# A two-memory attention kernel: a quad's sums stored in one transfer and read back in pieces, with new delays in the instruction plan

## The chip, the cores and the metric

The kernel runs on one core of a Trainium2 chip. A core has a matrix engine (TensorE, PE in the profile, its weight loads PEld), a vector engine (VectorE, DVE), an activation engine (ScalarE, ACT), a general engine (GpSimd, POOL) and SyncE (SP), which here does nothing but issue transfers to the core's 16 DMA engines. Each engine works through its own instruction stream strictly in order, and the streams are tied together by semaphores. The metric is the device time of one execution in microseconds; the median of the runs is given.

## What is computed

Two branches A and B get the same input `x` (2048 tokens, 640 features) with weights of their own. Each is an attention with 32 heads of 20 features over four segments of 512 tokens, together with a memory that is carried from segment to segment. The outputs are mixed by a gate per token.

```python
def _A_ref(x, wq, wk, wv, wo, beta):          # _B_ref is the same with B's weights
    H = 32; Dh = D // H; N = 4; L = S // N
    q, k, v = ...                              # x @ wq, x @ wk, x @ wv, by head and segment
    phi = lambda t: jnp.where(t > 0, t + 1.0, jnp.exp(t))
    mask = (ar[:, None] < ar[None, :]) * (-1e9)
    g = _sigmoid(beta).reshape(1, H, 1, 1)
    for s in range(N):
        logits = jnp.einsum("bhqd,bhkd->bhqk", qs, ks) * scale + mask
        p = _softmax(logits, axis=-1)
        a_dot = jnp.einsum("bhqk,bhkd->bhqd", p, vs)
        num = jnp.einsum("bhld,bhde->bhle", phi(qs), M)
        den = jnp.einsum("bhld,bhd->bhl", phi(qs), z)[..., None] + 1e-6
        outs.append(g * (num / den) + (1.0 - g) * a_dot)
        M = M + jnp.einsum("bhld,bhle->bhde", phi(ks), vs)
        z = z + jnp.einsum("bhld->bhd", phi(ks))
    return o @ wo

g = _sigmoid((x * gate_w).sum(-1, keepdims=True))
return g * a + (1 - g) * b
```

## The kernel before

**Units of work.** The work is cut into eight windows `t`: segment `t // 2` of branch `t % 2`. In a window stand the products of q, k and v with their weights (`job_qk`, `job_v`, 15 terms each, since every factor is split into a high and a low part), and the output product of the window before (`job_o`). All of these are issued on line 748. The 32 heads of a window are taken four at a time: eight quads `u`, 64 quads in all, `i = 8 t + u`. A quad has score products with queries in the rows (`s_unit`, line 1182), whose row maxima VectorE finds (line 1169); the maxima are turned around (line 1207) and written back beside the queries by two small transfers (line 1219). Then come score products with keys in the rows (`t_unit`, line 1272), whose exponentials ScalarE takes (line 1264) and GpSimd masks (line 1265), and the sums over the keys (`pv_unit`, line 1292). All products land in eight PSUM banks, each of which is free again when VectorE or ScalarE has read it. TensorE is used as two halves of 64 rows that work side by side.

**A quad's sums.** `pv_unit` leaves a tile `oT` of 128 rows and 512 tokens: for each of the four heads 20 rows of sums, one row with the sum of the exponentials (the denominator), and 11 rows of no use, 32 rows per head. In windows 0 to 6, `send_dot` writes it to DRAM: the four denominator rows to `dens` (line 1337) and the 20 rows of each head to `dots` (line 1339), five transfers, so that `dots` holds 640 rows without gaps. When half of the heads of a window are there, `reciprocals` reads their denominators back as a tile `dn` (line 1382), VectorE multiplies them with the gates and takes reciprocals (lines 1362 and 1364), and the result goes out (`recs`, line 1367) and is spread to 20 rows per head (`wide`, line 1372). `mix` then reads 128 rows of `dots` (line 1408) and of `wide` (line 1409), multiplies them (line 1406 on VectorE or 1407 on GpSimd) and splits the product for the output product. 35 such mixes are made, five per window.

**What sets the order.** Every engine's order is made when the program is built, by a small event model inside the kernel. It keeps a clock, a ready list per engine sorted by priority, and two numbers for the DMA engines. `put` charges an instruction its duration; `dma` charges SyncE for the issue and calls what comes behind the transfer after an assumed delay:

```python
    def dma(us, emit, then=None, prio=5, lat=1.1, some=False):

        def issued():
            dma_free[0] = max(clk[0] + 0.9, dma_free[0]) + us
            if not some:
                dma_free[0] = dma_free[1] = max(dma_free[0], clk[0] + 0.9 + us, dma_free[1] + us)
            if then:
                at(dma_free[0] + lat, then)

        put("S", 0.37, emit, issued, prio)
```

An instruction is written into its engine's stream when the model says that its inputs are there. If the transfer takes longer on the chip, the engine stands at that instruction, and all that is written behind it waits too. The table `RULES` holds eight settings per quad (the order of score units, how far ahead of the steady work they are spread, and some thresholds). `window_jobs` lists a window's products: `HEAD` holds the first five of the next window (q0, k0, q1, k1, q2); two of them stand ahead of the output products of the window before, three behind.

Weights come in through three tiles `wst` (line 546 for q, k and o, line 522 for v), are rounded by ScalarE (lines 538 and 512) and their low parts taken by GpSimd (lines 540 and 515). Tiles of `x` transposed come in by line 568 (ScalarE reads them on line 558), rows of `x` for the gate by line 613 (VectorE reads them on line 603).

## Time and profile before

| | us |
|---|---|
| runs shown, lowest, median, highest | 1056.81, 1060.92, 1069.14 |
| the profiled execution, its own time | 1060.1 |
| its span, first to last instruction | 1058.4 |
| mean granted TensorE clock | 0.997 |

The profile comes from one execution. An engine's "busy" is the time with at least one instruction in flight. A row of the waits names an engine and the line that stood waiting, what ended the wait, and then the total in us, the number of times and the longest. SyncE's rows ("SPq") give the time in which it issues; when a transfer lands, they don't tell. A row of the chain or of the timeline begins with start and length in us. In a row of windows stand the window, its length, and the busy time of each engine with its count of instructions, then the clock, the share of the DMA engines that is busy, and GB/s. The page counts 1301 transfers issued by SyncE.

### The profile page before, as it was taken

To read this page: it belongs to the slowest core of one execution; us is meant where nothing else is said; L and a number is where in the kernel's file an instruction comes from. 1 tells how busy PE (TensorE), PEld (TensorE's weight loads), DVE (VectorE), ACT (ScalarE), POOL (GpSimd) and SP (SyncE) were. 2 spreads that over 40 slices of the span, in tenths; PEclk is the share of its full clock that TensorE was granted. 3 is DMA by queue.
4 is the path that set the end of the run, shared out by engine and by line. 5 is a ranking of instruction groups with operands and counts; after the bars stand their busy time and mean duration, and the time that the engine had idled before them with its cause. 6 is when DMAs were issued, how large, how long until landed. Compare 5 with 4: busy or idle time off the path is not lost.

```text
span 1058.4 us, 31354 instructions
## 1 busy us (share of the span) xinstructions
PE 1013.3 (96%) x11260; PEld 853.4 (81%) x11260; DVE 768.8 (73%) x2642; ACT 658.2 (62%) x1338; POOL 582.9 (55%) x1016
## 2 busy tenths in 40 slices
PE   9998989899999999899999999999999999999998
PEld 7987877787988878777797888878888787787885
DVE  4777767577786768776778767887577886788864
ACT  6376656747576575656767557665575665658572
POOL 4454546546375563655737357475573644647362
PEclk9999999999999999999999999999999999999999
DMA  7996878787787779876767777887777877878631
GB/s 258 295 287 191 269 226 256 210 253 253 211 264 231 238 226 281 242 224 198 242 197 243 243 237 236 253 263 244 227 233 230 271 222 242 278 209 283 167 123 63
DMA packets 137307, 246.50 MB, mean 233 GB/s; under 512 B 21456, under 2 KB 25584, under 8 KB 137152
## 3 DMA queue, kind: packets, MB, share of 16 engines
q1 hardware_dynamic: 137152, 244.50, 75.6%
q8 instruction: 89, 1.46, 0.6%
q14 instruction: 66, 0.54, 0.2%
HBM read 159.88 MB, written 92.91 MB: 239 GB/s over the span
## 4 chain that ended last, share of the span: by engine, by line
PE 69%; DMA 16%; DVE 4%; ACT 3%; issue 3%; POOL 2%; SPq 2%; DVEq 0%; ACTq 0%; POOLq 0%
PE bank L748 40%; PE bank L1292 10%; PE bank L1182 6%; PE bank L1272 5%; DMA row<-wide 3%; DMA dn<-dens 2%; DMA kd<-row 2%; PE bank L938 2%; PE bank L858 2%; PE bank L898 2%; DMA row<-in_xT_dram 2%; ACT p L1264 1%; DMA qst<-qd 1%; DVE bank L1169 1%; DMA wst<-in_b_wk_dram 1%
## 5 line engine op out<-in xcount | busy, mean ns | idle before, releaser
L1169 DVE CUSTOM_DVE_ANT_0 bank<-bank,tri 128x512 f32<-128x512 f32 (+3 forms) x1024 | 474.4, 520 | 138.2 <-PE bank L1182 117.7
L748 PE MATMUL bank<-row,wh 64*128 64x512 f32 x2308 | 502.6, 403 | 0.1
L1264 ACT ACTIVATE p<-bank 128x512 f32<-128x512 f32 x576 | 316.5, 598 | 133.7 <-PE bank L1272 108.7
L1265 POOL TENSOR_SCALAR_AFFINE_SELECT p<-p 128x256 f32<-128x256 f32 (+1 forms) x576 | 215.6, 384 | 229.8 <-ACT p L1264 219.1
L748 PEld LDWEIGHTS bank<-row,wh 64*128 64x128 f32 x2308 | 320.7, 186 | 13.8 <-issue 1.2
L748 PE MATMUL bank<-row,wl 64*128 64x512 f32 x1154 | 297.1, 401 | 0.0
L540 POOL TENSOR_TENSOR wl<-wst,wh 128x640 fp32r<-128x640 f32 x115 | 179.7, 1566 | 79.5 <-ACT wh L538 75.3
L1182 PE MATMUL bank<-kst,qst 60*128 60x384 f32 (+3 forms) x1024 | 178.3, 320 | 14.7 <-ACT p L1264 5.3
L748 PE MATMUL bank<-wvh,row 64*128 64x320 f32 x1280 | 188.5, 316 | 0.9 <-DVE mx L1169 0.4
L1272 PE MATMUL bank<-qst,kst 62*128 62x512 f32 (+3 forms) x1024 | 174.6, 318 | 14.8 <-DVE mx L1169 5.2
L748 PEld LDWEIGHTS bank<-row,wl 64*128 64x128 f32 x1154 | 173.4, 186 | 5.3 <-issue 0.4
L748 PEld LDWEIGHTS bank<-wvh,row 64*128 64x128 f32 x1280 | 154.0, 186 | 4.8 <-ACT p L1264 1.1
L1182 PEld LDWEIGHTS bank<-kst,qst 60*128 60x128 f32 x1024 | 130.7, 186 | 28.0 <-ACT p L1264 9.2
L1272 PEld LDWEIGHTS bank<-qst,kst 62*128 62x128 f32 x1024 | 130.8, 186 | 24.1 <-DVE mx L1169 6.5
L1292 PE MATMUL bank<-p,vst 128*32 128x256 f32 (+3 forms) x1908 | 144.6, 426 | 1.8 <-DVE mx L1169 1.4
L1169 DVE DVE_READ_ACCUMULATOR2_ANT mx<- 128x1 f32 x1024 | 144.7, 141 | 0.0
L1292 PEld LDWEIGHTS bank<-p,vst 128*32 128x32 f32 x1908 | 59.1, 110 | 86.1 <-issue 62.1
L538 ACT CAST wh<-wst 128x640 fp32r<-128x640 f32 x119 | 87.1, 740 | 40.0 <-PE bank L748 10.5
L748 PE MATMUL bank<-wvl,row 64*128 64x320 f32 x640 | 107.2, 312 | 0.0
L748 PEld LDWEIGHTS bank<-wvl,row 64*128 64x128 f32 x640 | 84.8, 185 | 0.3
L515 POOL TENSOR_TENSOR wvl<-wst,wvh 128x640 fp32r<-128x640 f32 (+1 forms) x48 | 64.0, 1337 | 32.9 <-ACT wvh L512 30.9
L715 DVE TENSOR_TENSOR row<-bank,row 128x512 fp32r<-128x512 f32 x80 | 54.3, 686 | 28.2 <-ACT row L708 14.4
(117 smaller groups left out, 1154.9 us busy)
## 6 DMA issues: line engine op xcount, KB each, us to landing
qd<-row SPq DMA_DIRECT2D x120, 256.0 KB
kd<-row SPq DMA_DIRECT2D x120, 256.0 KB
qst<-qd SPq DMA_DIRECT2D x128, 240.0 KB
kst<-kd SPq DMA_DIRECT2D x128, 240.0 KB
dots<-row SPq DMA_DIRECT2D x224, 40.0 KB
wide<-recs SPq DMA_DIRECT2D x14, 640.0 KB
row<-dots SPq DMA_DIRECT2D x35, 256.0 KB
row<-wide SPq DMA_DIRECT2D x35, 256.0 KB
```

The source lines that it names most:

```text
L515: put("G", 0.77 * n, lambda: nc.gpsimd.tensor_tensor(out=wl[:, a:b, :], in0=w3, in1=r32(wh[:, a:b, :]), op=ALU.subtract), end, prio=4)
L538: put("A", 0.625, lambda: nc.scalar.copy(wh, w3), lambda: put(lo_eng, lo_cost, lambda: lo.tensor_tensor(out=wl, in0=w3, in1=r32(wh), op=AL ...
L540: lambda: lo.tensor_tensor(out=wl, in0=w3, in1=r32(wh), op=ALU.subtract), end, prio=3), prio=6)
L715: put("D", 0.605, lambda: nc.vector.tensor_tensor(out=lo, in0=src, in1=r32(hi), op=ALU.subtract), out, prio=1)
L748: return nc.tensor.matmul(bank_of, lhsT=w[ROWS[half]], rhs=x_[ROWS[half]], start=start, stop=stop)
L858: return nc.tensor.matmul(pm[:, a - h0:c - h0, :].rearrange("p h e -> p (h e)"), lhsT=r32(pqTs[t, m][ROWS[half], P * n:P * (n + 1)]), rhs= ...
L1169: put("D", w / 960.0 + 0.105, lambda: nc.vector.tensor_tensor_reduce(out=sc[:, off:off + w], in0=sc[:, off:off + w], in1=tri[:, L - w:], s ...
L1182: lane_ops[half].append((mm(w), lambda pair=pair, qb=qb, off=off, w=w, r=r, sc=sc: nc.tensor.matmul(sc[:, off:off + w], lhsT=q[r, pair, P ...
L1264: put("A", 0.483, lambda: nc.scalar.activation(pt, sc, AF.Exp, scale=SCALE), lambda: (bank.give(sc), put("G", 0.15 + 0.105 * len(todo), la ...
L1265: "G", 0.15 + 0.105 * len(todo), lambda: nc.gpsimd.affine_select(out=blocks, in_=blocks, pattern=[[0, len(todo)], [1, P]], base=0, channel ...
L1272: lane_ops[half].append((mm(w), lambda pair=pair, kb=kb, off=off, w=w, r=r, sc=sc: nc.tensor.matmul(sc[:, off:off + w], lhsT=k[r, pair, P ...
L1292: nc.tensor.matmul(po[32 * j:32 * j + 32, P * kb:], lhsT=vst[t % 2][:, kb, h * E1:h * E1 + 32], rhs=pts[i, n, f][0][:, off:off + w], start ...
```

## The change

Four things are changed.

1. `send_dot` writes the whole tile `oT`, 128 rows, in one transfer. `dots` has 1024 rows instead of 640 (32 per head), and `dens` is gone; `reciprocals` reads the denominators as every 32nd row of `dots`.
2. `mix` gathers its 128 rows in pieces: one transfer for the whole heads among them, and one for the part of a head at either end. For the five mixes of a window these are 2, 3, 3, 3 and 2 pieces, 13 in place of 5.
3. The model charges an issue 0.44 us in place of 0.37 (0.63 to 0.69 for some kinds), and assumes longer delays: `lat` 2.0 in place of 1.1 for weights, for x tiles of segments 1 to 3, for the token rows and for `dn`, 1.8 for both reads of a mix, 1.6 for the gate rows, 1.4 for `recs`.
4. Three products of the next window stand ahead of the output products, not two. The table `RULES` has new numbers in nearly all of its rows.

```diff
     RULES = {
-        0: "STTSTSSTST 0.902 2.38 0.24 8 0.0 0.78 1",
+        0: "TSTSTSTSTS 1.010 1.98 0.35 8 0.0 1.6 1.92",
...
-    def dma(us, emit, then=None, prio=5, lat=1.1, some=False):
+    def dma(us, emit, then=None, prio=5, lat=1.1, some=False, issue=0.44):
...
-        put("S", 0.37, emit, issued, prio)
+        put("S", issue, emit, issued, prio)
...
-    dots = [dram.tile([D, L], F32, name=f"dots{i}") for i in range(7)]
-    dens = [dram.tile([H, L], F32, name=f"dens{i}") for i in range(7)]
+    dots = [dram.tile([32 * H, L], F32, name=f"dots{i}") for i in range(7)]
...
-        got += ahead[:2]
+        got += ahead[:3]
         if t > 0:
             got += [(t - 1, "o", m) for m in range(KT)]
-        got += ahead[2:]
+        got += ahead[3:]
...
-            dma(0.84, lambda: nc.sync.dma_start(out=w3, in_=src[m]), landed, prio=0 if i < 4 else need[i])
+            dma(0.84, lambda: nc.sync.dma_start(out=w3, in_=src[m]), landed, prio=0 if i < 4 else need[i], lat=1.1 if i < 4 else 2.0)
...
-        one = then_all(5, sent)
-        dma(0.1, lambda: nc.sync.dma_start(out=dens[t][4 * u:4 * u + 4, :], in_=oT[DH::32, :]), one, prio=-1)
-        for j in range(4):
-            dma(0.12, lambda j=j: nc.sync.dma_start(
-                out=dots[t][80 * u + DH * j:80 * u + DH * (j + 1), :], in_=oT[32 * j:32 * j + DH, :]), one, prio=-1)
+        dma(0.7, lambda: nc.sync.dma_start(out=dots[t][P * u:P * u + P, :], in_=oT), sent, prio=-1)
...
         dma(0.1, lambda: nc.sync.dma_start(
-            out=d, in_=dens[t][rows, :].rearrange("h (a n) -> (h a) n", n=SPAN)), landed, prio=-1)
+            out=d, in_=dots[t].rearrange("(h r) (a n) -> h r a n", r=32, n=SPAN)[rows, DH, :, :]), landed, prio=-1, lat=2.0)
...
-        landed = then_all(2, lambda: anyof(
+        parts_of, f = [], P * k
+        while f < P * k + P:
+            h, e = divmod(f, DH)
+            n = (P * k + P - f) // DH if e == 0 else 0
+            if n:
+                parts_of.append((f - P * k, n * DH, dots[t].rearrange("(h r) n -> h r n", r=32)[h:h + n, :DH, :]))
+                f += n * DH
+            else:
+                n = min(DH - e, P * k + P - f)
+                parts_of.append((f - P * k, n, dots[t][32 * h + e:32 * h + e + n, :]))
+                f += n
+
+        landed = then_all(1 + len(parts_of), lambda: anyof(
...
-        dma(0.7, lambda: nc.sync.dma_start(out=r32(y), in_=dots[t][P * k:P * k + P, :]), landed, prio=0)
-        dma(0.7, lambda: nc.sync.dma_start(out=r32(r), in_=wide[t][P * k:P * k + P, :]), landed, prio=0)
+        for f, n, src in parts_of:
+            dma(0.0055 * n, lambda f=f, n=n, src=src: nc.sync.dma_start(out=r32(y[f:f + n, :]), in_=src), landed, prio=0, lat=1.8)
+        dma(0.7, lambda: nc.sync.dma_start(out=r32(r), in_=wide[t][P * k:P * k + P, :]), landed, prio=0, lat=1.8)
```

The changed kernel's lines lie three to eight further up (748 is 744, 1182 is 1178, 1362 is 1354), those of the mix four or five further down (1406 is 1410, 1408 is 1413). SyncE issues 1133 transfers where it issued 1301; the number of products is the same.

How this moves instructions is shown at two places. The first is the first two mixes of window 0, on SyncE. Before, with a quad's five writes ahead of them (`kst`, `qst`: score operands; `row`: a tile of 128 rows and 512 tokens; `mr`: the maxima):

```order
L1337 DMA dens0_124<-row5_3024_2538 4x512
L1339 DMA dots0_117<-row5_3024_2538 20x512
L1219 DMA qst0_80<-mr1_190 2x8x128 x2
L1339 DMA dots0_117<-row5_3024_2538 20x512 x3
L546 DMA wst0_166<-in_a_wo_dram 128x640
L1140 DMA qst3_83<-qd1_98 60x2x512 x2
L1140 DMA kst3_87<-kd1_106 60x2x512
L1408 DMA row18_3218_2667<-dots0_117 128x512
L1409 DMA row27_3219_2668<-wide0_138 128x512
L1408 DMA row23_3223_2669<-dots0_117 128x512
L1409 DMA row8_3224_2670<-wide0_138 128x512
```

And the same place on SyncE now:

```order
L1332 DMA dots0_117<-row16_2945_2541 128x512
L1136 DMA qst3_83<-qd1_98 60x2x512 x2
L1136 DMA kst3_87<-kd1_106 60x2x512 x2
L564 DMA row23_3122_2654<-in_xT_dram 128x512
L1413 DMA row19_3162_2682<-dots0_117 120x1x512
L1413 DMA row19_3162_2682<-dots0_117 8x512
L1414 DMA row16_3163_2683<-wide0_131 128x512
L1413 DMA row8_3189_2703<-dots0_117 12x512
L1413 DMA row8_3189_2703<-dots0_117 100x1x512
L1332 DMA dots0_117<-row25_3198_2709 128x512
L1413 DMA row8_3189_2703<-dots0_117 16x512
L1414 DMA row14_3190_2704<-wide0_131 128x512
```

Five issues of a quad have become one; a mix's two reads have become three and four, and its last read, of `wide`, stands behind its pieces.

The second place is the read of the denominators `dn` of the second half of window 2's heads. On VectorE before (rows of two: a scan of one block of scores and the read of its maxima):

```order
L1169 ISA bank5_163,mx26_6832<-bank5_163,tri_69 128x384
L1169 ISA mx26_6832 128x1
L1169 ISA bank2_160,mx26_6832<-bank2_160,tri_69 128x384
L1169 ISA mx26_6832 128x1
L1169 ISA bank5_163,mx26_6832<-bank5_163,tri_69 128x128
L1169 ISA mx26_6832 128x1
L1362 SCALAR_TENSOR_TENSOR dn1_192<-dn1_192,gcol0_156,rg2_182 128x64
L1364 RECIPROCAL dn1_192<-dn1_192 128x64
L1169 ISA bank2_160,mx26_6832<-bank2_160,tri_69 128x128
L1169 ISA mx26_6832 128x1
```

And on VectorE now (L711, L694 and L695 finish a product with k):

```order
L1165 ISA bank1_152,mx26_6827<-bank1_152,tri_69 128x128
L1165 ISA mx26_6827 128x1
L711 TENSOR_TENSOR row9_8697_6990<-bank7_158,row25_8696_6989 128x512
L1165 ISA bank1_152,mx26_6827<-bank1_152,tri_69 128x512
L1165 ISA mx26_6827 128x1
L694 TENSOR_SCALAR bank7_158<-bank7_158 128x512
L1354 SCALAR_TENSOR_TENSOR dn1_185<-dn1_185,gcol0_149,rg2_175 128x64
L1356 RECIPROCAL dn1_185<-dn1_185 128x64
L695 TENSOR_TENSOR row8_8698_6991<-bank7_158,row8_8698_6991 128x512
```

Between the issue of `dn` and its reader VectorE had eight scans of scores before; now it has ten and two other operations of 512 columns.

More of the change, by code (lines that the diff above doesn't have):

```diff
@@ L568, in got @@
             dma(0.7, lambda: nc.sync.dma_start(
-                out=r32(st), in_=xT[P * k:P * (k + 1), L * s:L * (s + 1)]), landed, prio=need[job_index[2 * s, "q", 0]] - 4 * (s > 0))
+                out=r32(st), in_=xT[P * k:P * (k + 1), L * s:L * (s + 1)]), landed, prio=need[job_index[2 * s, "q", 0]] - 4 * (s > 0), lat=2.0 if s else 1.1)
         big.want((F32R, F32R, F32), got, prio=4, spare=SPARE if s else 0)
@@ L650, in spread @@
                 0.2, lambda: nc.sync.dma_start(out=r, in_=rows_g[t].rearrange("h (a n) -> (h a) n", n=SPAN)),
-                lambda: (row_gate.__setitem__(t, r), dots_ready(t)), prio=8, some=True), prio=8, some=True)
+                lambda: (row_gate.__setitem__(t, r), dots_ready(t)), prio=8, some=True, lat=1.6), prio=8, some=True, issue=0.63, lat=1.6)
     gates_asked = []
@@ L1221, in send @@
                         in_=r32(mr[16 * half:16 * half + 16, :]),
-                    ), done, prio=-2, some=True)
+                    ), done, prio=-2, some=True, issue=0.68)
             put("A", 0.15, lambda: nc.scalar.copy(mr, b[:32, :P]), send, prio=1)
@@ L1367, in written @@
             dma(0.1, lambda: nc.sync.dma_start(
-                out=recs[t][rows, :].rearrange("h (a n) -> (h a) n", n=SPAN), in_=d), widen, prio=-1)
+                out=recs[t][rows, :].rearrange("h (a n) -> (h a) n", n=SPAN), in_=d), widen, prio=-1, some=True, lat=1.4)
         def widen():
@@ L1373, in widen @@
                 out=wide[t][DH * 16 * g:DH * 16 * (g + 1), :].rearrange("(h e) n -> h e n", e=DH),
-                in_=recs[t][rows, None, :].to_broadcast([16, DH, L])), over, prio=-1)
+                in_=recs[t][rows, None, :].to_broadcast([16, DH, L])), over, prio=-1, issue=0.69)
         def over():
```

4 lines of the change are left out of this document (2 added, 2 removed), and 113 rows, old and new, of the table RULES.

## The prediction

> **What bounds the kernel now.** I read the page first: span, busy shares, DMA queue, chain.
>
> ```profile
> span 1058.4 us, 31354 instructions
> PE 1013.3 (96%) x11260; PEld 853.4 (81%) x11260; DVE 768.8 (73%) x2642; ACT 658.2 (62%) x1338; POOL 582.9 (55%) x1016
> q1 hardware_dynamic: 137152, 244.50, 75.6%
> PE 69%; DMA 16%; DVE 4%; ACT 3%; issue 3%; POOL 2%; SPq 2%; DVEq 0%; ACTq 0%; POOLq 0%
> ```
>
> TensorE has a matmul in flight for 1013.3 of 1058.4 us, and the change takes no matmul away. So what it can win from idle time is at most 1058.4 - 1013.3 = 45.1 us. The chain's 16% for DMA must not be read as a prize of 170 us: the chain charges a transfer's whole flight, and during most of it TensorE worked on something else. The groups of PE say where its idle time stands.
>
> ```profile
> L1182 PE MATMUL bank<-kst,qst 60*128 60x384 f32 (+3 forms) x1024 | 178.3, 320 | 14.7 <-ACT p L1264 5.3 <-DVE mx L1169 4.5 <-DMA kst<-kd 1.4
> L1272 PE MATMUL bank<-qst,kst 62*128 62x512 f32 (+3 forms) x1024 | 174.6, 318 | 14.8 <-DVE mx L1169 5.2 <-DVE row L699 3.0 <-ACT p L1264 3.0
> L1207 PE MATMUL bank<-ident,mt 64*32 64x64 f32 x128 | 28.2, 220 | 4.7 <-POOL mt L1194 4.5 <-ACT row L1264 0.2
> ```
>
> 34.2 of the 45.1 us lie ahead of score products (L1182, L1272) and of the row of maxima (L1207), and hardly any (1.4 us in these rows) is ended by a DMA. TensorE waits for a bank that VectorE or ScalarE has not emptied. Yet those two are only 73% and 62% busy. So I asked what they themselves wait for, and took out every row that a load or read-back ended.
>
> ```profile
> DVE row L1406 <- DMA row<-wide: 22.9, 18, 3.8
> ACT wvh L512 <- DMA wst<-in_b_wv_dram: 18.4, 14, 3.1
> ACT row L558 <- DMA row<-in_xT_dram: 15.0, 8, 4.9
> DVE dn L1362 <- DMA dn<-dens: 13.6, 11, 4.0
> DVE wst L603 <- DMA wst<-in_x_dram: 8.3, 4, 5.5
> ACT wvh L512 <- DMA wst<-in_a_wv_dram: 7.9, 7, 2.8
> POOL row L1407 <- DMA row<-wide: 7.7, 3, 3.9
> ACT wh L538 <- DMA wst<-in_a_wq_dram: 6.0, 7, 2.1
> ACT wh L538 <- DMA wst<-in_b_wq_dram: 5.0, 4, 2.7
> ACT wh L538 <- DMA wst<-in_b_wk_dram: 4.6, 3, 3.4
> ACT wh L538 <- DMA wst<-in_a_wk_dram: 4.1, 3, 2.2
> ```
>
> Columns: total us, times, longest. Together 113.5 us in 82 stalls, 1.4 us each. The engines run in the order that the plan wrote, so one early reader holds up all that stands behind it. The timeline shows one such place:
>
> ```profile
> 438.12 0.42 SPq L1382 DMA_DIRECT2D dn<-dens  x1
> 443.21 0.28 DVE L1362 SCALAR_TENSOR_TENSOR dn<-dn,gcol,rg 128x64 f32<-128x64 f32 x1 [4.04 <-DMA dn<-dens]
> 440.95 0.62 ACT L558 CAST row<-row 128x512 fp32r<-128x512 f32 x1 [3.25 <-DMA row<-in_xT_dram]
> 442.12 0.50 PE L1182 MATMUL bank<-kst,qst 60*128 60x512 f32 x2 [2.43 <-ACT p L1264]
> ```
>
> The reader of `dn` starts 5.09 us after its issue, where the plan before allows 0.9 + 0.1 + 1.1 = 2.1 us. VectorE stands for 4.04 us, ScalarE for 3.25 us on an x tile, and TensorE runs out of banks for 2.43 us. I followed each PE gap over 0.25 us back in this way. Fifteen places lead to a load or read-back; these are the first, the last and the sum of their windows (length, PE busy, ...):
>
> ```profile
> 80.00:85.00 5.00, 2.25 (x24) 1.68 (x21) 3.89 (x9) 2.25 (x7) 1.45 (x1) 1.00 1.02 240
> 952.00:956.00 4.00, 1.70 (x18) 1.49 (x16) 2.39 (x11) 3.05 (x6) 2.26 (x3) 1.00 0.16 40
> sum 59.00, PE 36.50 PEld 28.38 DVE 38.09 ACT 38.52 POOL 36.20; mean PE 2.43 PEld 1.89 DVE 2.54 ACT 2.57 POOL 2.41
> ```
>
> So 59.0 - 36.5 = 22.5 us of TensorE's idle time come from late transfers: 22.5 / 113.5 = 0.20 us per us of stall. Short stalls are absorbed by the eight banks, long ones come through nearly whole.
>
> **The change, part by part.** *The plan's delays.* This is the part that pays. Loads of weights, x and token rows are now expected 0.9 us later, `dn` 0.9 us, the pair of a mix 0.7 us, and SyncE is charged 0.44 us or more per issue, not 0.37. The readers move back in their engines' orders. I counted in both orders how much TensorE work is emitted between an issue and its first reader, each product at the pace of these rows of the chain (512 columns, 320 columns, quad sums):
>
> ```profile
> 219.16 2.69 PE bank L748 x22
> 977.09 1.78 PE bank L748 x23
> 1003.01 2.29 PE bank L1292 x32
> ```
>
> That is 0.12, 0.08 and 0.07 us a matmul. Reads with under 3.5 us of work ahead of them fall from 8 to 1 of 14 for `dn`, from 21 to 5 of 48 for value weights, from 4 to 2 of 16 for token rows, from 6 to 4 of 120 for the other weights. For x of the later segments they stay at 4 of 15 (under 4.5 us: 9 to 7), for the mix's `wide` rows at 8 of 35 (under 4.5 us: 16 to 12). The medians move by +1.5 us (`dn`), +1.1 (value weights), +0.7 (x), +0.5 (token rows) and +0.3 (other weights, mixes). Taking these shifts off the stalls above:
> - `dn`: 13.6 us in 11 stalls, mean 1.2; less 1.5 each leaves about 2 (the one of 4.0). -11.6.
> - value weights: 26.3 in 21, mean 1.25; less 1.1 leaves about 8. -18.
> - token rows 8.3: one stall of 5.5 stays mostly. -3.
> - x: 15.0, two large stalls; -4.
> - other weights: 19.7, some of it at the very start, where nothing moves; -6.
> - mixes: 22.9 + 7.7 = 30.6; -3, see below.
>
> In all -46 of 113.5 us. At 0.20 this is -9 us of TensorE idle time. Bounds: 0, if the plan only moves the hole (what stood behind the reader now stands ahead of another one), and -22.5, if every late transfer is covered.
>
> *Sums in one transfer.* The queue's own rows give SyncE's price of each form (min/median/max ns):
>
> ```profile
> L1339 SPq DMA_DIRECT2D dots<-row x224: 272/330/1626, 70.9 to 952.8; - x112
> L1337 SPq DMA_DIRECT2D dens<-row x56: 515/550/824, 68.6 to 947.1; - x56
> L1408 SPq DMA_DIRECT2D row<-dots x35: 326/422/1447, 165.2 to 969.3; - x35
> L1372 SPq DMA_DIRECT2D wide<-recs x14: 581/587/619, 132.8 to 960.1; - x14
> ```
>
> Removed: 224 x 0.330 + 56 x 0.550 = 104.7 us of issuing, and the 35 reads, 14.8 us. Added: 56 whole-tile writes at the 0.422 of L1408, 23.6 us; 91 pieces, of which 35 (100 or 120 rows out of a strided source) have the look of `wide` and are taken at 0.587, 20.5 us, and 56 (4 to 16 rows) look like the 20-row writes, 0.330, 18.5 us. The 14 `dn` reads become strided, +2.3 us. Net -55 us of SyncE. None of it lies on TensorE's path by itself, but SyncE is in order, so what stood behind five issues of a quad (1.9 us) is issued 1.4 us sooner: weight and x loads, score operands. At most this cures as much again as half of the stalls left, (113.5 - 46) / 2 x 0.20 = 7 us; at least it does nothing, as the plan held those issues back anyway. I take -3, nearer to nothing, because SyncE's own longest wait is for other engines, and a queue that comes sooner to such a wait gains nothing there:
>
> ```profile
> SPq L1140 <- PE bank L1272: 38.3, 26, 6.3
> ```
>
> *More bytes.* A tile of 128 rows leaves where 84 rows did: 44 x 2 KB x 56 = 5 MB on 244.5, +2%. The queue has room on the mean (75.6%), but the first window above stands at 1.02 of all engines. 0 to +3 us; I take +1.
>
> *Output product behind three products.* 3.7 us (30 half products at 0.12) more between a mix and its first use. TensorE's products (L748) don't idle in the trace, so I cost this at 0; the cover is the next segment's loads and splits, which have to be there one product earlier. If they are not, one product's 3.7 us per segment is the price, seven times at most, but the reads of these weights have over 10 us of work ahead of them in the median in both orders.
>
> *The table of rules.* It reorders everything finely and has no row of its own. I take 0 and give it +-8 us. The measure for that is the sum of the windows of six more idle places, which I could not trace to a transfer, 23.0 - 13.8 = 9.2 us:
>
> ```profile
> sum 23.00, PE 13.78 PEld 9.28 DVE 16.20 ACT 10.09 POOL 13.46; mean PE 2.30 PEld 1.55 DVE 2.70 ACT 1.68 POOL 2.24
> ```
>
> Sum: -9 - 3 + 1 = -11. Against the profiled execution's 1060.1 us (span 1058.4 and 1.7 around it) this gives 1049; the median of the runs shown is 1060.92, 0.8 above it, which is nothing here.
>
> **The rivals.** *The hole moves* (no change). For it: the six untraced places, and that x and mix reads, 45.6 of the 113.5 us, hardly gain distance. Against it: `dn` and value weights clearly do. If only these pay, and half of that turns up as new holes, (11.6 + 18) x 0.20 / 2 = 3 us: 1057.
>
> *The pieces land late* (slower). A mix needs all of its pieces and blocks VectorE until then. One busy engine of the queue moves 244.5 MB / (0.756 x 16 x 1058.4 us) = 19.1 KB/us. A whole tile of 262 KB over 16 engines is 0.86 us. Suppose that a piece of six heads spreads over no more engines than it has heads: its 246 KB take 2.14 us, 1.3 more. Two or three mixes follow each other in SyncE's order, so the third would be up to 3.9 us late: 35 mixes x 2 us = 70 us of stall. At 0.20 that is +14, and at 0.5, since these would be long stalls, +35: 1063 to 1084, 1073 in the middle. It decides from about 1.5 us per mix. Against it: the large piece is issued about 1 us ahead of the `wide` row that closes the pair, and `wide` is often what ends the wait today. No row of this profile shows over how many engines a piece spreads.
> The Trainium skill (DMA: Bandwidth & Descriptors, section on why a DMA increments its semaphore by 16) says that the number of engines is the largest up to 16 that divides the outermost counts of both sides, which for 6 heads of 20 rows is 6. By that rule this rival's first price holds and the forecast would be 1063 at least. No run here shows it yet.
>
> *All of it goes.* If the new table also closes the untraced places, -22.5 - 7: 1031. Nothing in the rows speaks for the large stalls (5.5, 4.9 us) going too.
>
> **How the numbers follow.** Forecast, late readers moved and half cured, 1041 to 1051: 0.40. All of it, below 1041: 0.12. The hole moves, 1051 to 1066: 0.34. Late pieces, above 1066: 0.14. The predicted time is 1049. The range leaves out 0.1 on each side: from 1037 to 1069. A measurement of this kernel can tell about 1% (10.6 us): faster than 1050.3 takes in "all of it" and most of the forecast, 0.50; slower than 1071.5 most of the late pieces, 0.12; the same, 0.38.
>
> **What would show it.** Right: the stalls of `dn` and of the value weights' casts fall under 3 and 10 us; PE's idle time ahead of L1182's and L1272's successors falls from 29.5 to about 20; SyncE's rows show 56 writes near 0.42 us. Wrong: the mix's rows on VectorE and POOL wait for pieces of `dots` rather than for `wide`, and more than 45 us in all (late pieces); or the stalls fall and PE's idle time does not (the hole moved). An x cast or a score operand that ends most of PE's idle time would be a wait that I have not priced.

## The result, and the profile after

| | before | changed |
|---|---|---|
| median of 20 runs each, us | 1061.24 | 1054.74 |
| lowest to highest, us | 1052.38 to 1071.16 | 1050.12 to 1061.13 |
| ratio, 95% interval | | 0.9941 (0.9921 to 0.9961) |
| profiled execution, its own time and span, us | 1060.1, 1058.4 | 1050.84, 1049.1 |
| its mean granted clock | 0.997 | 0.989 |

The change wins 0.6%, by the interval 4.1 to 8.4 us. By the 1% bound of the prediction that is "the same", the case given 0.38 and not the likeliest one. The time lies 5.7 us above the forecast and inside the range. How it comes about is another matter than the sum that I wrote down, and most of what follows is on that.

From the page of the changed kernel, the span, the busy times, the DMA queue and the chain by engine:

```profile
span 1049.1 us, 31149 instructions
PE 1014.1 (97%) x11260; PEld 858.9 (82%) x11260; DVE 758.6 (72%) x2632; ACT 661.2 (63%) x1344; POOL 582.6 (56%) x1020
q1 hardware_dynamic: 138244, 249.54, 77.5%
PE 70%; DMA 16%; DVE 4%; SPq 4%; ACT 2%; issue 2%; POOL 2%; DVEq 0%; ACTq 0%; POOLq 0%
```

TensorE's time without a matmul in flight fell from 45.1 us to 1049.1 - 1014.1 = 35.0 us. From the groups, its two kinds of score products:

```profile
L1268 PE MATMUL bank<-qst,kst 62*128 62x384 f32 (+3 forms) x1024 | 180.9, 323 | 17.8 <-DVE mx L1165 7.0
L1178 PE MATMUL bank<-kst,qst 60*128 60x384 f32 (+3 forms) x1024 | 181.3, 318 | 5.4 <-DVE mx L1165 3.3
```

Their idle time fell from 29.5 to 23.2 us. The rows of the waits that answer to the eleven shown before:

```profile
DVE row L1410 <- DMA row<-wide: 35.9, 19, 3.6
ACT wvh L508 <- DMA wst<-in_b_wv_dram: 12.9, 7, 3.0
POOL row L1411 <- DMA row<-wide: 7.6, 3, 3.7
ACT row L554 <- DMA row<-in_xT_dram: 7.6, 8, 3.1
DVE dn L1354 <- DMA dn<-dots: 4.6, 3, 3.1
ACT wvh L508 <- DMA wst<-in_a_wv_dram: 4.4, 3, 1.9
ACT wh L534 <- DMA wst<-in_a_wk_dram: 4.0, 4, 2.3
ACT wh L534 <- DMA wst<-in_b_wq_dram: 3.0, 3, 1.8
ACT wh L534 <- DMA wst<-in_a_wq_dram: 2.6, 3, 1.7
DVE wst L599 <- DMA wst<-in_x_dram: 1.6, 3, 0.9
ACT wh L534 <- DMA wst<-in_b_wk_dram: 1.2, 1, 1.2
```

They make 85.4 us, where they made 113.5. Without the two rows of the mixes the fall is from 82.9 to 41.9 us. The mixes themselves wait for longer than before, 43.5 us instead of 30.6 (45.1 with one wait of 1.6 us that names a piece). And SyncE's new rows (min/median/max ns of an issue):

```profile
L1332 SPq DMA_DIRECT2D dots<-row x56: 319/343/609, 69.9 to 928.8; - x56
L1413 SPq DMA_DIRECT2D row<-dots x91: 264/482/959, 158.3 to 957.5; - x91
```

### The profile page after: what moved, and what is told of

Its sections match the earlier page's. It is cut to its first block, busy times and chain, and to the rows that moved or that the text cites. A ratio compares the mean times of both kernels' runs of the same rounds, so it can differ in the third digit from the quotient of the medians.

```text
span 1049.1 us, 31149 instructions
## 1 busy us (share of the span) xinstructions
PE 1014.1 (97%) x11260; PEld 858.9 (82%) x11260; DVE 758.6 (72%) x2632; ACT 661.2 (63%) x1344; POOL 582.6 (56%) x1020
## 3 DMA queue, kind: packets, MB, share of 16 engines
q1 hardware_dynamic: 138244, 249.54, 77.5%
## 4 chain that ended last, share of the span: by engine, by line
PE 70%; DMA 16%; DVE 4%; SPq 4%; ACT 2%; issue 2%; POOL 2%; DVEq 0%; ACTq 0%; POOLq 0%
PE bank L744 41%; PE bank L1288 11%; PE bank L1268 6%; PE bank L1178 6%; DMA row<-wide 4%; PE bank L934 2%; PE bank L854 2%; PE bank L894 2%; SPq L1413 2%; DVE bank L1165 2%; DMA wst<-in_b_wv_dram 1%; DMA qd<-row 1%; DMA qst<-qd 1%; DMA row<-dots 1%; DMA kst<-kd 1%
## 5 line engine op out<-in xcount | busy, mean ns | idle before, releaser
L1165 DVE CUSTOM_DVE_ANT_0 bank<-bank,tri 128x384 f32<-128x384 f32 (+3 forms) x1024 | 475.3, 520 | 155.2 <-PE bank L1178 119.1
L744 PE MATMUL bank<-row,wh 64*128 64x512 f32 x2308 | 503.8, 404 | 1.1 <-DVE row L701 1.1
L1260 ACT ACTIVATE p<-bank 128x512 f32<-128x512 f32 x582 | 319.9, 600 | 138.8 <-PE bank L1268 102.7
L744 PEld LDWEIGHTS bank<-row,wh 64*128 64x128 f32 x2308 | 318.4, 186 | 13.6 <-DVE row L701 1.3
L744 PE MATMUL bank<-row,wl 64*128 64x512 f32 x1154 | 304.7, 401 | 0.0
L536 POOL TENSOR_TENSOR wl<-wst,wh 128x640 fp32r<-128x640 f32 x115 | 180.1, 1570 | 66.2 <-ACT wh L534 64.1
L1268 PE MATMUL bank<-qst,kst 62*128 62x384 f32 (+3 forms) x1024 | 180.9, 323 | 17.8 <-DVE mx L1165 7.0
L1178 PE MATMUL bank<-kst,qst 60*128 60x384 f32 (+3 forms) x1024 | 181.3, 318 | 5.4 <-DVE mx L1165 3.3
L744 PE MATMUL bank<-wvh,row 64*128 64x320 f32 x1280 | 184.8, 316 | 0.7 <-DVE mx L1165 0.7
L744 PEld LDWEIGHTS bank<-row,wl 64*128 64x128 f32 x1154 | 178.3, 187 | 5.5
L1268 PEld LDWEIGHTS bank<-qst,kst 62*128 62x128 f32 x1024 | 132.6, 188 | 30.3 <-DVE mx L1165 10.2
L744 PEld LDWEIGHTS bank<-wvh,row 64*128 64x128 f32 x1280 | 153.3, 187 | 2.6 <-DVE mx L1165 0.9
L1178 PEld LDWEIGHTS bank<-kst,qst 60*128 60x128 f32 x1024 | 133.6, 187 | 15.3 <-DVE mx L1165 5.9
L744 PE MATMUL bank<-wvl,row 64*128 64x320 f32 x640 | 105.3, 313 | 0.0
L534 ACT CAST wh<-wst 128x640 fp32r<-128x640 f32 x119 | 87.0, 742 | 28.1 <-PE bank L744 14.0
L744 PEld LDWEIGHTS bank<-wvl,row 64*128 64x128 f32 x640 | 84.3, 186 | 0.2
L1318 ACT COPY row<-bank 128x512 f32<-128x512 f32 x55 | 32.5, 592 | 56.2 <-PE bank L1288 45.8
```

What stands on the lines that cost most here:

```text
L534: put("A", 0.625, lambda: nc.scalar.copy(wh, w3), lambda: put(lo_eng, lo_cost, lambda: lo.tensor_tensor(out=wl, in0=w3, in1=r32(wh), op=AL ...
L536: lambda: lo.tensor_tensor(out=wl, in0=w3, in1=r32(wh), op=ALU.subtract), end, prio=3), prio=6)
L744: return nc.tensor.matmul(bank_of, lhsT=w[ROWS[half]], rhs=x_[ROWS[half]], start=start, stop=stop)
L1165: put("D", w / 960.0 + 0.105, lambda: nc.vector.tensor_tensor_reduce(out=sc[:, off:off + w], in0=sc[:, off:off + w], in1=tri[:, L - w:], s ...
L1178: lane_ops[half].append((mm(w), lambda pair=pair, qb=qb, off=off, w=w, r=r, sc=sc: nc.tensor.matmul(sc[:, off:off + w], lhsT=q[r, pair, P ...
L1260: put("A", 0.483, lambda: nc.scalar.activation(pt, sc, AF.Exp, scale=SCALE), lambda: (bank.give(sc), put("G", 0.15 + 0.105 * len(todo), la ...
```

## The experiments

Two counts are used in what follows that no view gives. *Idle of a half*: each matmul of the trace, taken in order, is matched with the program's, which says on which 64 rows it works; the time in which a half has none in flight, between its first matmul and its last, is summed, and the mean of both halves taken; it is good to about 1 us. (The page's PE row calls TensorE busy when one half works.) *Time at half clock*: the sum of the stretches in which the granted clock stood at 0.5, without the one that begins behind the last matmul. And one number is of the building, not of the chip: *the plan's own end*, the clock of the model when it wrote the last instruction. "Stalls" are all idle times of VectorE, ScalarE and GpSimd that a transfer ended, not only those of the eleven rows.

| kernel | median us | ratio to before | plan's own end | median less plan | stalls | idle of a half | at half clock |
|---|---|---|---|---|---|---|---|
| before | 1061.2 | | 1001.2 | 60.1 | 125.4 | 51.0 | 6.8 |
| changed | 1054.7 | 0.994 (0.992 to 0.996) | 1003.8 | 51.0 | 112.7 | 41.6 | 20.5 |
| e1, old plan, new transfers | 1080.7 | 1.016 (1.013 to 1.019) | 1001.2 | 79.5 | 148.5 | 64.1 | 30.7 |
| e2, new plan, old transfers | 1057.4 | 0.994 (0.992 to 0.997) | 1003.8 | 53.6 | 109.7 | 44.7 | 10.2 |
| e9, large piece first | 1056.6 | 0.996 (0.993 to 0.999) | 1003.8 | 52.8 | 99.2 | 45.8 | 23.9 |
| c1, before, weights 1.15 | 1078.9 | 1.014 (1.010 to 1.019) | 1023.5 | 55.4 | 130.8 | 59.3 | 34.1 |
| c2, before, issue 0.38 | 1119.0 | 1.055 (1.049 to 1.060) | 1052.1 | 66.9 | 142.8 | 77.9 | 51.2 |
| e4, changed, weights 2.05 | 1095.7 | 1.030 (1.027 to 1.034) | 1054.7 | 41.0 | 101.6 | 71.6 | 37.5 |
| c3, changed, weights 1.95 | 1090.4 | 1.026 (1.023 to 1.029) | 1057.5 | 32.9 | 78.7 | 61.8 | 47.8 |
| e7, changed, old table | 1091.6 | 1.028 (1.022 to 1.033) | 1042.4 | 49.2 | 106.4 | 64.8 | 34.1 |
| e5, changed, mixes 3.0 | 1089.0 | 1.023 (1.018 to 1.028) | 1037.4 | 51.6 | 99.0 | 67.3 | 37.5 |
| e8, as e5, table searched anew | 1071.3 | 1.009 (1.006 to 1.012) | 1013.0 | 58.3 | 126.2 | 52.6 | 27.3 |

**The plan and the transfers apart.** In e1 every engine but SyncE has before's order row by row, and SyncE has before's slots; only what is transferred there is the change's.

```diff
-        dma(0.1, lambda: nc.sync.dma_start(out=dens[t][4 * u:4 * u + 4, :], in_=oT[DH::32, :]), one, prio=-1)
+        dma(0.1, lambda: nc.sync.dma_start(out=dots[t][P * u:P * u + P, :], in_=oT), one, prio=-1)
...
+            dma(0.12, lambda: None, one, prio=-1)
...
-        dma(0.7, lambda: nc.sync.dma_start(out=r32(y), in_=dots[t][P * k:P * k + P, :]), landed, prio=0)
+        dma(0.7, pieces, landed, prio=0)
```

> The kernel before with the changed transfers and nothing else: a quad's sums leave in one transfer in the place of the first of the five, the mix's pieces are issued in the place of its one read, the denominators are read with a stride. The orders of TensorE, VectorE, ScalarE and GpSimd are those of before, row by row. Theory 'the plan's delays pay, the transfers cost': 1.000 to 1.006 of before, stalls of VectorE and GpSimd at the mixes (L1406, L1407) up from 30.6 us to over 40, all other stalls on loads within 15 us of before. Rival 'SyncE's relief pays': 0.992 to 0.996 of before with no new delay in the plan, stalls on weights and x down by 10 us or more.

It is 1.6% slower than before, in the direction of the first theory and well beyond its 1.000 to 1.006. The waits of its mixes, from the view of waits:

```profile
DVE row L1420 <- DMA row<-wide: 41.5, 20, 3.8
POOL row L1421 <- DMA row<-wide: 9.9, 3, 4.3
```

That is 51.4 us instead of 30.6, and two rows of mixes that wait for pieces (3.4 and 3.6 us) come on top: 27.8 us more in 35 mixes, 0.8 each. What one such wait sets off, the timeline of e1 shows (start, length, engine, line, what it does, and in brackets the idle time ahead):

```profile
465.08 1.27 POOL L1421 TENSOR_TENSOR row<-row,row 128x512 f32<-128x512 f32 x1 [3.65 <-DMA row<-dots]
470.87 1.26 POOL L1421 TENSOR_TENSOR row<-row,row 128x512 f32<-128x512 f32 x1 [1.80 <-DMA row<-wide]
471.39 0.62 ACT L557 CAST row<-row 128x512 fp32r<-128x512 f32 x1 [6.94 <-DMA row<-in_xT_dram]
473.55 0.43 POOL L1193 TENSOR_TENSOR mt<-mx,mt 128x16 fp32r<-128x16 f32 x1 [0.20 <-ACT mt L1192]
474.04 0.29 PE L1206 MATMUL bank<-ident,mt 64*32 64x64 f32 x1 [3.38 <-POOL mt L1193]
```

GpSimd stands for 3.65 and 1.80 us on two mixes, ScalarE for 6.94 us on an x tile; the maxima of a quad pass through both, they come late, and TensorE stands for 3.38 us. The 27.8 us of stall cost 17.7 us of time, 0.64 per us. Part of that is the clock: over e1's six runs the mean granted clock is 0.977 to 0.986, median 0.984, over the 17 runs of before beside them 0.985 to 0.998, median 0.990. The difference of 0.0065 is some 7 us of 1080.

In e2 it is the other way round: the orders of the changed kernel, in its slots the five writes and the one read of before.

```diff
-        dma(0.7, lambda: nc.sync.dma_start(out=dots[t][P * u:P * u + P, :], in_=oT), sent, prio=-1)
+        dma(0.7, five, sent, prio=-1)
...
+            dma(0.0055 * n, lambda f=f: f or nc.sync.dma_start(out=r32(y), in_=dots[t][P * k:P * k + P, :]), landed, prio=0, lat=1.8)
```

> The changed kernel with the transfers of before: five writes of a quad's sums in the place of the one, one read of 128 rows in the place of a mix's first piece. The orders of the four compute engines are those of the changed kernel. Theory 'the plan's delays pay, the transfers cost': 0.988 to 0.994 of before, at or below the changed kernel; stalls at the mixes (L1410, L1411 in the changed kernel) down from 43 us to under 33. Rival 'SyncE's relief pays': 0.998 to 1.002 of before.

```profile
ACT wvh L509 <- DMA wst<-in_b_wv_dram: 18.4, 13, 3.3
DVE row L1416 <- DMA row<-wide: 11.1, 9, 2.7
DVE dn L1360 <- DMA dn<-dens: 9.6, 6, 3.2
DVE wst L600 <- DMA wst<-in_x_dram: 8.2, 6, 2.1
POOL row L1417 <- DMA row<-wide: 4.7, 3, 2.2
```

It is as fast as the changed kernel within the intervals, which leave some 3 us either way. So the gain is the plan's, and the transfers are worth nothing that can be told under this plan. The stalls fit that: with the old transfers the mixes wait for 15.8 us, not 43.5, but value weights, `dn` and token rows wait for longer than in the changed kernel (18.4, 9.6 and 8.2 against 12.9, 4.6 and 1.6 us), and for `dn` the trace shows that SyncE comes to it later: the shortest time from its issue to a VectorE that is free to read it is 1.7 us in e2, 2.6 us in the changed kernel. What the pieces lose, 45.1 - 15.8 = 29.3 us of stall, the saved issues win. Under the old plan the pieces lost as much, 27.8 us, and little fell in return: all stalls rose by 23.1 us, here by 3.0.

**The transfers by themselves.** m1 has none of the computation: one transfer after another, each followed by a copy on VectorE that needs it. The short edit that matters:

```diff
+    def whole():
+        nc.sync.dma_start(out=y, in_=flat[0:P, :])
+    def six():
+        nc.sync.dma_start(out=y[0:120, :], in_=heads[0:6, :DH, :])
```

> Not the kernel: transfers alone, one after the other, each read by VectorE before the next is issued; the attention is left out and the output is not written with it. A whole tile of 128 rows, 120 rows of six heads, 100 rows of five heads, 8 rows, and a mix's three pieces; then a quad's sums in one write and in five. If a piece spreads over only as many engines as it has heads, 120 and 100 rows take 1.0 to 1.6 us longer from issue to reader than the whole tile. If it spreads over all, they take at most 0.3 us longer.

```profile
30.89 0.35 SPq L80 DMA_DIRECT2D y<-flat  x1
33.57 0.17 DVE L99 COPY z<-y 128x8 f32<-128x8 f32 x1 [2.71 <-DMA y<-flat]
33.98 0.75 SPq L83 DMA_DIRECT2D y<-dots  x1
38.49 0.17 DVE L99 COPY z<-y 120x8 f32<-120x8 f32 x1 [4.55 <-DMA y<-dots]
```

From the issue to the reader a whole tile takes 33.57 - 30.89 = 2.68 us, a piece of six heads, which has fewer bytes, 38.49 - 33.98 = 4.51 us, and its issue holds SyncE for 0.75 us instead of 0.35. Over all repetitions the piece takes 4.41 to 4.61 us, a piece of 8 rows 1.61 to 1.71. The difference of 1.83 us is beyond the expected 1.0 to 1.6, but not all of it is flight. Windows from the first to the last byte of the same two transfers (window, length, VectorE, GpSimd, the clock, DMA share, GB/s):

```profile
31.89:33.19 1.30, 0.00 (x0) 0.00 (x0) 1.00 0.73 202
35.52:38.10 2.58, 0.00 (x0) 0.00 (x0) 1.00 0.33 95
```

The bytes of the piece move for 1.28 us longer; the rest passes before the first byte, with the longer issue. On the mean the whole tile keeps 0.73 x 16 = 11.7 engines busy, the piece 5.3, as fits six engines and not sixteen. A strided source that is slow row by row is ruled out as the cause: a packet of 2 KB takes 84 ns (median) in both.

**Is the table fitted to one order?** Four kernels move one number that carries no idea, and a fifth takes back the table alone.

```diff
+            ... landed, prio=0 if i < 4 else need[i], lat=1.1 if i < 4 else 2.05)
```

> The changed kernel with one number of the plan touched: the delay assumed for the weights of q, k and o is 2.05 us, not 2.0. That is nothing in itself, but it reorders most of the plan. Theory 'the delays pay': 0.990 to 0.998 of before, as the changed kernel is. Rival 'the table of rules is fitted to one plan, and what was gained is that fit': 1.000 or above; the distance to the changed kernel is then the size of the plan's own scatter.

```diff
+            ... landed, prio=0 if i < 4 else need[i], lat=1.1 if i < 4 else 1.15)
```

> The kernel before with one number moved: the assumed delay of the weights of q, k and o 1.15 us, not 1.10. It carries no idea; about two thirds of the rows of every engine stand elsewhere. Theory F (the table of rules is fitted to one order, in this kernel as in the changed one): what the fit had won is lost, as where the changed kernel was nudged by 0.05 us (1.030): 2 to 3.5% slower than before, 1082 to 1098, with the idle time of each half of TensorE up by 12 to 25 us while the stalls on loads stay within 20 of before's 113.5. Rival D (the delays decide, and the other nudge was an accident): within 1% of before, 1051 to 1071.

```diff
-        put("S", 0.37, emit, issued, prio)
+        put("S", 0.38, emit, issued, prio)
```

> The kernel before with SyncE's charge per issue 0.38 us, not 0.37, which reorders nearly everything. Theory F (a fitted table): 2 to 3.5% slower than before, 1082 to 1098. Rival D (the delays decide): within 1% of before, 1051 to 1071. With the nudge of the weights' delay this gives two orders of the kernel before that its table was not made for; their mean is what its delays are worth without a fit.

```diff
+            ... landed, prio=0 if i < 4 else need[i], lat=1.1 if i < 4 else 1.95)
```

> The changed kernel with the delay of the weights of q, k and o 1.95 us, not 2.00. Theory F (a fitted table): like the nudge to 2.05, 2 to 3.5% slower than before, 1080 to 1098, although the stalls on loads stay near the changed kernel's (about 75 us) or below. Rival D (the delays decide): within 1% of the changed kernel, 1044 to 1065.

```diff
     RULES = {
-        0: "TSTSTSTSTS 1.010 1.98 0.35 8 0.0 1.6 1.92",
+        0: "STTSTSSTST 0.902 2.38 0.24 8 0.0 0.78 1",
...
```

> The changed kernel with the table of rules of before: transfers, charges, delays and the place of the output product are as changed, the 66 settings are not. Theory F (the gain needs a table fitted to the new order): 2 to 4% slower than before, 1080 to 1103, the idle time of each half of TensorE 60 to 80 us, though the stalls on the denominators and the value weights stay as low as in the changed kernel (4.6 and 17.5 us, each within 8). Rival D (the delays give the gain by themselves, the table next to nothing): 1045 to 1062, at or below before.

All five are slower than before, by 1.4 to 5.5%, whichever kernel was nudged. Theory F holds; of its four ranges two are met (c3, e7), c1 falls 3 us short and c2 goes 21 us beyond. c1's halves stand for 8 us longer than before's, where 12 to 25 were expected. The plan's own end says it already: it goes from 1001 to 1004 with a table made for the order, to 1023 to 1058 without. The stalls do not show it. c3 has the fewest of all, 78.7 us, and is 2.6% slower than before. Its halves stand one at a time, and part of its time runs at half clock; the page's first row hides both. In e4's they show only as a busy time that is 39.5 us longer than the changed kernel's for the same 11260 matmuls:

```profile
PE 1053.6 (96%) x11260; PEld 885.9 (81%) x11260; DVE 762.2 (70%) x2635; ACT 663.9 (61%) x1346; POOL 578.4 (53%) x1015
```

These kernels also show, in part, what the delays do without a fit. With before's delays (c1, c2) the plan ends at 1023.5 and 1052.1 and the chip takes 55.4 and 66.9 us more. With the new ones (e4, c3, e7, e5) it ends at 1037.4 to 1057.5, and the chip takes 32.9 to 51.6 more. With the longer delays a plan is some 10 us longer by its own clock (means 1037.8 and 1048.0) and the chip overruns it by some 17 us less (61.2 and 43.7). That is two orders against four, scattered by 20 to 30 us, and the four also have the new transfers, the higher charges and the other place of the output products. The signs are as longer delays would have them; that the delays alone make them is not shown.

**A still longer delay for the mixes.** If the pieces need more time than the plan gives them, more delay should cure the mixes' 43.5 us. For e8 the table was searched anew, by the plan's own end alone.

```diff
-            ... landed, prio=0, lat=1.8)
+            ... landed, prio=0, lat=3.0)
```

> The changed kernel with the assumed delay of a mix's reads 3.0 us, not 1.8, and the table of rules as it was, so not fitted to this order. Theory O (the time is the plan's own end plus an overrun that goes with the stalls on transfers, 0.60 us per us less 16, as over the nine kernels so far): the plan's own end is 1037.4 (changed kernel 1003.8); the mix's stalls of 43.5 us fall to about 10, all stalls from 113 to about 80, the overrun to 32 (28 to 42): 1069 (1065 to 1080). Rival T (the overrun is a constant, some 51 us, whatever the stalls are): 1088. Rival M (a mix's late pieces cost nothing under this plan, and the longer delay neither): 1050 to 1060.

> The same delay of 3.0 us with a table of rules searched for this order, which brings the plan's own end from 1037.4 to 1013.0; the changed kernel's is 1003.8, so this plan is the worse by 9.2 us by its own clock. Theory O: stalls on transfers about 80 us, overrun 32 (26 to 42), so 1045 (1039 to 1055), 0.98 to 0.994 of before and about 10 us below the changed kernel. Rival T (a constant overrun of 51 us): 1064, the changed kernel plus 9. Rival M (late pieces cost nothing): 1060 to 1066.

Both miss theory O's times, by 20 and 26 us, and my reason falls: the mixes still wait, 26.3 us in e5 and 31.2 in e8, where I expected about 10. Rival T's constant overrun meets e5 (1088) and misses e8 by 7; rival M misses e5 by 29 and the end of its range for e8 by 5. The waits of e8, its mixes and the largest of those on score operands:

```profile
DVE row L1417 <- DMA row<-wide: 17.6, 9, 4.6
POOL row L1418 <- DMA row<-wide: 13.6, 5, 6.1
POOL wl L543 <- DMA kst<-kd: 8.1, 1, 8.1
ACT wh L541 <- DMA kst<-kd: 5.7, 1, 5.7
PE bank L1185 <- DMA kst<-kd: 4.3, 3, 2.9
```

In e8 the readers of a mix that have to wait start 3.3 to 8.2 us after the issue of `wide`, in the changed kernel 3.7 to 7.6; alone, in m1, a whole tile took 2.7. So the time that the transfers take is not fixed, and one longer delay does not cover it; what it grows with is not shown. And the new table has waits of its own: the 8.1 and 5.7 us that are put down to `kst` end at 38.5 and 44.6 us, long before the first mix (L543 and L541 work on weights, so that name too may be only that of the last transfer). What held, roughly, is the relation between stalls and overrun: by the rule in the expectation (0.60 per us less 16), the stalls measured, 99.0 and 126.2, give overruns of 43 and 60; measured were 51.6 and 58.3.

**The order within a mix.** The slots and all compute orders stay as changed; the large piece takes the first slot, `wide` the next.

```diff
+        for us, (n, dst, src) in zip(costs, sorted(loads, key=lambda x: -x[0])):
+            dma(us, lambda dst=dst, src=src: nc.sync.dma_start(out=r32(dst), in_=src), landed, prio=0, lat=1.8)
```

> The changed kernel with the same slots on SyncE for each mix, filled in another order: the large piece first, then the row of wide, then the small pieces. The orders of TensorE, VectorE, ScalarE and GpSimd are the same row by row. Theory P (the long flight of a large piece, 4.4 to 4.6 us alone against 2.7 of a whole tile and 1.6 of a small piece, decides when a mix may start): in about 22 of 35 mixes the large piece is issued 0.3 us sooner, in all the row of wide 0.3 to 0.75 us sooner; the mix's stalls fall from 43.5 to about 36 us, and the time by 0.6 per us, 4 us, to about 1050 (0.988 to 0.992 of before). Rival Q (the load of the DMA engines decides, not the order within a mix): stalls of 41 to 46 us, time 1053 to 1057.

```profile
DVE row L1410 <- DMA row<-dots: 34.8, 20, 4.3
POOL row L1411 <- DMA row<-wide: 1.5, 1, 1.5
```

The stalls fall to 36.3 us as expected, and their name changes: the rows "row<-wide" had named the transfer issued last, not the slow one. The time does not follow: 1056.6, where theory P said 1050, with an interval that holds the changed kernel's ratio. Rival Q has the time right (1053 to 1057) and the stalls wrong (41 to 46). So 7 us off these stalls, and 13.5 off all stalls, are worth less than the run can resolve: the relation between stalls and overrun holds over kernels with different orders, and does not price a single stall. No kernel here beats the changed one; e2 and e9 equal it.

**Gaps and the clock.** In the changed kernel's trace the granted clock falls to half right behind a gap. Windows of 3.41 us around one (window, length, PE busy, PEld, VectorE, ScalarE, GpSimd, the clock, DMA share, GB/s):

```profile
924.60:928.01 3.41, 3.41 (x48) 1.75 (x46) 1.54 (x5) 1.68 (x4) 1.29 (x3) 1.00 0.87 223
928.02:931.43 3.41, 1.57 (x24) 1.27 (x22) 1.54 (x4) 1.28 (x3) 0.51 (x1) 1.00 1.02 278
931.43:934.84 3.41, 3.41 (x23) 3.17 (x25) 3.41 (x13) 2.28 (x5) 1.52 (x2) 0.50 0.39 124
934.84:938.25 3.41, 3.41 (x41) 3.41 (x41) 2.42 (x10) 2.21 (x6) 1.73 (x4) 1.00 0.51 148
```

TensorE stands for 1.84 us of the second window; in the third it has a matmul in flight all the time and starts 23, in the first it started 48. m2 sets such gaps on purpose.

```diff
+            for i in range(48):
+                nc.tensor.matmul(bank, lhsT=w, rhs=m, start=True, stop=True)
+            nc.vector.tensor_copy(z, bank[:, 0:8])
+            for i in range(k):
+                nc.vector.tensor_copy(y, oT)
+            nc.vector.tensor_copy(w, oT[:, 0:P])
```

> Not the computation: only gaps of TensorE and the granted clock. 60 groups of 48 matmuls (128 rows, 512 columns) wait for each other through one to six copies on VectorE, so that TensorE stands for some 1 to 4 us between groups; the output gets a constant. Theory G (a fixed grid of windows of 3.41 us; where TensorE stands for over about 1.75 us of one window, the next runs at half clock): gaps under 1.7 us never bring a drop, gaps of 2.0 us do in some 55% and of 2.5 us in some 70% (the others are split over two windows), gaps over 3.5 us always; and each drop starts within 3.41 us of the gap's end. Rival L (only a gap longer than a window brings a drop): none for gaps under 3.4 us. Rival R (the drops are chance, or go with other engines): no relation to the length.

Two gaps of the same length, 2.11 us, in m2 (no ScalarE column here):

```profile
245.27:248.68 3.41, 1.43 (x7) 0.85 (x5) 1.84 (x6) 0.00 (x0) 1.00 0.00 0
248.68:252.09 3.41, 3.28 (x8) 2.60 (x9) 0.08 (x1) 0.00 (x0) 0.50 0.00 0
327.18:330.59 3.41, 2.34 (x11) 1.61 (x9) 0.96 (x4) 0.00 (x0) 1.00 0.00 0
330.59:334.01 3.42, 2.38 (x10) 1.99 (x11) 0.95 (x3) 0.00 (x0) 1.00 0.00 0
334.01:337.42 3.41, 3.41 (x16) 2.81 (x15) 0.00 (x0) 0.00 (x0) 1.00 0.00 0
```

Of the first, 1.98 us lie in one window of the grid, and a window at 0.50 follows. The second is split over two, 1.08 and 1.03 us, and nothing happens. Of the 59 gaps, the 22 with 1.98 us or more in one window were all followed by a drop, the 37 with 1.76 us or less never. Theory G holds, with a limit between these two numbers. Its shares were off, 2 of 9 at 2.11 us and 10 of 10 at 2.57, since the gaps kept meeting the grid at like places; gaps over 3.1 us did not come about.

## Why the prediction came out as it did

*The ceiling.* "At most 45.1 us" was the wrong sort of bound. It counts the time in which neither half has a matmul, 5.8 us of it ahead of the first matmul and behind the last. The halves' own idle time between these two was 51.0 us, and half clock is lost time inside the busy time. Over all twelve kernels, the span less the idle of a half less half of the time at half clock is 997 to 1011 us, while the spans themselves reach from 1049 to 1115. For the two profiled executions the parts are -9.4 us (halves), +6.8 (clock: 20.5 - 6.8, halved) and -6.7 that these two counts do not explain; together the -9.3 of the spans. The clock's part belongs to these two executions: over 58 runs of before the granted clock lies between 0.985 and 0.998, median 0.990, and over the changed kernel's 20 the median is 0.989.

*The plan's delays*, -46 us of stall at 0.20, -9 us. This is the step in which two errors cancelled, by luck. The stalls of the eleven rows fell by 28.1 us, not 46. `dn` fell by 9.0 (I had 11.6), value weights by 9.0 (18), token rows by 6.7 (3), x by 7.4 (4), the other weights by 8.9 (6): -41.0 against -43, well met in sum, with the value weights overrated twofold. The mixes, at -3, rose by 12.9; e2 shows that the plan alone takes them from 30.6 to 15.8, and the pieces put 29.3 back. The price per us was too low instead: PE's idle time fell by 10.1 us for 28.1, 0.36 per us. Over the twelve kernels the median less the plan's own end goes with all stalls by 0.53 us per us (correlation 0.91; the largest miss 7.4 us).

*Sums in one transfer*, -55 us of SyncE, -3 us. SyncE's issuing fell from 598.6 to 547.2 us by its rows, so -51. What it is worth, with the pieces and the 5 MB (249.54 - 244.50) taken together, is e2 against the changed kernel: ratios of 0.994 and 0.994, zero, where my two terms gave -2. But that zero is 29.3 us of new stalls against 26 old ones cured, and under the old plan the same transfers cost 17 to 20 us (e1).

*Late pieces.* The rival's price of one flight was right: I supposed that a piece spreads over no more engines than it has heads, 1.3 us more; in m1 its bytes move for 1.28 us longer, and it arrives 1.8 later. The Trainium skill's rule (DMA: Bandwidth & Descriptors, section on why a DMA increments its semaphore by 16) gives six engines for such a piece; m1 agrees with it, 5.3 engines busy on the mean against 11.7 for the whole tile. What failed is the sum: I had 2 us per mix and 70 in all, the runs show 0.8 per mix; why so much of the flight is hidden was not measured. The price failed the other way: 0.2 to 0.5 per us of stall was my range, and under the old plan it was 0.64. I put the point from which it decides at 1.5 us per mix; at 0.64 per us it is 11 / (35 x 0.64) = 0.5. And whether it costs anything hangs on the plan, which I had not seen: at 0.8 us per mix it cost 1.6% under the old plan and nothing under the new.

*Output product behind three*, 0. TensorE stood for 1.8 us ahead of its products (L744) in the changed kernel. This step was not tried alone, since it cannot be moved without reordering everything behind it.

*The table of rules*, 0 +- 8. This is the term that was sized from the wrong thing. With the same delays and transfers, before's table gives 1091.6 (e7), 37 us more. A nudge of 0.05 us or 0.01 us costs either kernel 18 to 58 us. Zero came out right as a net, because before's table had been as well made for its order: the plan's own ends are 1001.2 and 1003.8. The +- 8 from six untraced places had nothing to do with it; had the new table been a little less well made for its order, everything else in the sum would have been noise beside it. That the gain is the plan's is shown (e2). How it divides between delays and table is not: e7 and the nudges allow "delays -7, table even", and the scatter of unfitted orders allows much else.

*What would show it.* `dn` was to fall under 3 us and fell to 4.6; the value weights under 10 and fell to 17.3; the score products' idle time to about 20 and fell to 23.2; the whole-tile writes were to take 0.42 us and take 0.343. Of the signs against, the first came in part: the mixes' rows make 43.5 us, with the one that names a piece 45.1, at the mark of 45; most name `wide`, but e9 shows that the name misleads.

## What to carry to other kernels

Where a planner writes the orders and its table is searched, price a change of the planner first by its own end before and after, and only then by the waits: an unfitted order cost 1.4 to 5.5% here, the transfers 1.6% at most. Cheaper issuing and slower flights must be tried under the plan that they will run under, since the same transfers were worth nothing under one and cost 1.6% under the other. A wait for several transfers is named after the one issued last, so measure a new form of transfer alone before you blame the name.

## What the hardware showed that I had not expected

A pause of TensorE shorter than its clock's window can cost twice, once as a pause and once more as a window at half clock behind it. Over the twelve traces of the kernel, of the 3.41 us windows on the clock's grid in which the halves stood idle for 1.8 us or more (mean of both), 50 of 50 were followed by a drop to half clock; of those with 1.5 to 1.8 us 16 of 44, with 1.0 to 1.5 us 6 of 116, with less none of 3434 (windows that stood at half clock already are not counted). Most drops last 3.41 or 6.83 us, the longest 13.65. The Trainium skill (TensorE: Matmul & The Clock Gate, sections on what's actually happening and on oscillation in real kernels) describes a free-running window of 4096 cycles, 3413 ns, and the grid agrees with it. Its rule of thumb, no idle gaps over about 3.4 us, is too lax here: gaps of 2.11 us were enough in m2 when 1.98 us or more of them fell into one window, and never when 1.76 us or less did.

The overrun of a plan goes with the stalls, but a longer assumed delay removes only part of the stalls that it is meant for: with 3.0 us in place of 1.8 the mixes still waited for 26 to 31 us, where it had been 43.5.
